# A table of offsets on the due times that order the instructions of a fused top-k attention and MLP kernel

## The chip, the cores and the metric

One core of a Trainium2 chip runs the kernel. The metric is the device time of one execution in microseconds (us), median of several runs. TensorE is called PE below, VectorE DVE, ScalarE ACT, GpSimd POOL; SyncE (SP) issues all DMAs of the kernel from one queue.

## The reference

```python
def _attn_ref(q, k, v):                      # q, k, v: (4, 8, 576, 64) float32
    scores = 1/sqrt(64) * matmul(q, k.T)
    kth = the 32nd largest of each row
    scores = where(scores >= kth, scores, -1e9); attn = softmax(scores)
    return matmul(attn, v)
def _moe_ref(x, w_in, w_out):                # x: (2304, 512); w_in (512, 2048), w_out (2048, 512)
    h = x @ w_in
    return (h * sigmoid(1.702 * h)) @ w_out
def _moe2_ref(x, w1, w2, w3, w_out):         # w1, w2: (512, 1024); w3 (1024, 1024); w_out (1024, 512)
    return ((x @ w1) * (x @ w2) @ w3) @ w_out
def reference(...):
    x = attention, heads joined to (2304, 512)
    return _moe2_ref(_moe_ref(x))
```

The weights arrive as 64-bit floats, the rest as 32-bit floats.

## The kernel before, in words

**Work.** The 2304 tokens are 18 tiles of 128. A tile has 8 heads. A head (`head`) is: scores `S` on PE into one of two PSUM buffers `s_ps` (L760); four `max` (L782) and three `mr` (match and replace, L785) on DVE, which find the 32nd largest score; `nb` (L792), a 128x1 operation that may run on POOL or on DVE; `cut` and `exp` on ACT (L800, L803); a split of the result into two fp16 parts, `a hi` on ACT (L809) and `a lo` on POOL (L812, L813); a DMA transpose `a T` (L816, into `ats`); and `av` on PE (L823). `tile_end` normalises the tile and transposes it (`x T`, L905, into `tsb`).

A tile then goes through `moe`: `h` products with `win`, tanh and a multiplication by ACT and POOL, a transpose `g T` (L973), `x2` products with `wout`, a transpose `x2 T` (L1010), products `a` and `b` with `w12`, their product, a transpose `p T` (L1077), products `o` with `w34` (w3 and the last weight, multiplied beforehand), and a store. All these products run in halves of six 128x512 fp16 matmuls (`product_op`, L532 to L534), eight halves for `h`, eight for `x2`, four for each of `a`, `b` and `o`.

**Weights.** Beside the first tiles, `weights` prepares 72 blocks of 128x512 in five stages: the last weight (8 blocks), w3 (16), w_in (16), w_out (16), w1 and w2 (16). `load64` loads a block (`w load`, L372), makes a 32-bit float of it with two ACT operations (`w low` L377, `w main` L391), one that may run on ACT or on POOL (`w sign`, L387 or L382), and one on DVE (`w join`, L395). `l2_scale` sums squares on PE (`gram`, L422) and derives a scale in DVE steps (`diag` L432, `w scale` L440, L441, L445, L446). `split_pe` copies a block through PSUM and splits it by that scale: `w in` on PE (L459), `w hi` on ACT (L462), `w lo` on DVE (L465). The 64-bit blocks of a later stage are loaded into memory that the split of an earlier stage frees, so the stages form a chain.

**What sets the order.** Class `Order` holds every operation with a due time `prio`, the engines that it may run on (`alts`: engine, cost, function, a wait `w` before that engine is considered), its dependencies and the buffers it takes and returns. `run` goes through planned time, and each time an engine is free it takes, of the operations that are ready in its plan, the one with the smallest due time. The costs are numbers in the code (`cost` in `pe`, `dve`, `act`, `pool`, `dma`). What the chip sees is only the resulting order on each of the five queues: each engine executes its list in that order, and waits by semaphores for the data itself. The due times come from `head_due`, which gives head n a time, with constants added for each kind:

```python
def head_due(n):
    return 9.0 * min(n, 16) + 5.7 * max(n - 16, 0) + 12.0
```

`S` and `av` get this time less 1000, so that PE takes them before any product.

Of the kernel before, what the change touches and what calls it, by code (L numbers as in the profile page):

```python
# [35 lines left out]
class Order:  # L36
# [22 lines left out]
    def op(self, alts, due, deps=(), env=None, acq=(), rel=(), tag="", lat=None):  # L59
        o = Op()  # L60
        o.alts, o.prio, o.lat = alts, due, lat
        o.acq = [(a, env, a) if isinstance(a, str) else a for a in acq]
        o.rel = [(a, env, a) if isinstance(a, str) else a for a in rel]
        o.left, o.users, o.ready, o.end, o.why = 0, [], 0.0, None, None
        o.tag, o.seq, o.done = tag, len(self.ops), False
        for d in deps:
            if d is not None:
                d.users.append(o)
                o.left += 1
        self.ops.append(o)  # L70
        return o
# [98 lines left out]
SIGN_G = 0.5  # L170

# [6 lines left out]
def kernel(  # L178
# [120 lines left out]
    def pe(cost, due, fn, **kw):  # L299
        return op([("T", cost, fn, 0.0)], due, **kw)  # L300
# [444 lines left out]

    def head(t, h, X):
# [85 lines left out]
        s = pe(0.5 if len(pt) == 1 else 0.65, due - 1000 - 8, f_s, deps=qready[t] + kd, env=E, acq=["sp"], rel=rel, tag="S")  # L832
# [8 lines left out]
        for i in range(3):  # L841
# [13 lines left out]
            0.55 if len(pt) == 1 else 0.75, due - 1000 + 10, f_av, deps=[tr] + vd + [X["av op", h - 1] if j else None],  # L855
# [3 lines left out]
        X["av op", h] = av
# [80 lines left out]
    def moe(t, X):  # L940
# [8 lines left out]
        gs = []  # L949
        for j in range(NG):  # L950
# [3 lines left out]
                [X["xt"]] + ready["win"][4 * j : 4 * j + 4], [("mm", E, "mm")], [("t", X, "t")] if j == NG - 1 else [], "h",  # L954
# [68 lines left out]
        ps_, pd = [], []  # L1023
        for j in range(NP_):
# [3 lines left out]
                [x2t] + ready["w12"][4 * j : 4 * j + 4], [("mm", Ea, "mm")], [], "a",  # L1028
# [120 lines left out]
```

## Time and profile before

| | |
|---|---|
| median of 3 runs | 1120.21 us (1118.58 to 1121.06) |
| the profiled execution | 1122.92 us, span 1121.1 us |
| PE, DVE, ACT, POOL busy | 987.4, 938.6, 833.6, 755.6 us |
| mean granted PE clock | 0.975 of full speed |

The span runs from the first to the last instruction of the profiled execution; times in the rows count from its start. A view of waits says which engine and line waited for which other. An entry PEld is PE's weight load, which goes ahead of its matmul. SPq is the DMA queue.

### The profile page before, as it was taken

To read this page: it belongs to the slowest core of one execution; us is meant where nothing else is said; L and a number is where in the kernel's file an instruction comes from. 1 tells how busy PE (TensorE), PEld (TensorE's weight loads), DVE (VectorE), ACT (ScalarE), POOL (GpSimd) and SP (SyncE) were. 2 spreads that over 40 slices of the span, in tenths; PEclk is the share of its full clock that TensorE was granted. 3 is DMA by queue.
4 is the path that set the end of the run, shared out by engine and by line. 5 is a ranking of instruction groups with operands and counts; after the bars stand their busy time and mean duration, and the time that the engine had idled before them with its cause. 6 is when DMAs were issued, how large, how long until landed. Compare 5 with 4: busy or idle time off the path is not lost.

```text
span 1121.1 us, 18684 instructions
## 1 busy us (share of the span) xinstructions
PE 987.4 (88%) x5798; PEld 504.9 (45%) x5798; DVE 938.6 (84%) x2079; ACT 833.6 (74%) x1589; POOL 755.6 (67%) x1092
## 2 busy tenths in 40 slices
PE   1367898688879999999999998999999999999995
PEld 1233343344434445555445454454445555455442
DVE  4798899699799999989999878998998999997311
ACT  6987858988978776878788687777777777777421
POOL 6733332555547886989798887878879796776320
PEclk9998999879989999999999999999999999999998
DMA  7969958768746675786776859576865664746331
GB/s 236 293 151 229 257 101 221 197 138 177 160 113 110 128 132 118 127 167 115 136 143 122 155 103 156 107 131 124 134 140 97 135 136 94 144 83 122 76 57 38
DMA packets 428740, 156.96 MB, mean 140 GB/s; under 512 B 406624, under 2 KB 414816, under 8 KB 428640
## 3 DMA queue, kind: packets, MB, share of 16 engines
q1 hardware_dynamic: 428640, 155.78, 67.6%
q8 instruction: 45, 0.74, 0.3%
q14 instruction: 55, 0.45, 0.1%
HBM read 52.43 MB, written 4.72 MB: 51 GB/s over the span
## 4 chain that ended last, share of the span: by engine, by line
PE 38%; DVE 16%; DMA 14%; ACT 12%; POOL 12%; issue 7%; SPq 1%; POOLq 0%; ACTq 0%; DVEq 0%
PE mm L532 10%; PE mm L534 10%; PE mm L533 10%; DVE m8s L782 7%; DVE wsb L785 6%; DMA ats<-hlb 5%; DMA tsb<-hsb 5%; PE av L823 4%; PE s_ps L760 3%; POOL hsb L343 2%; POOL hlb L813 2%; ACT ysb L803 2%; POOL hsb L935 1%; ACT s_ps L800 1%; PE mm L459 1%
## 5 line engine op out<-in xcount | busy, mean ns | idle before, releaser
L782 DVE MAX8 m8s<-wsb 128x8 f32<-128x576 f32 x432 | 323.6, 755 | 5.3
L785 DVE MATCH_REPLACE8 wsb<-m8s,wsb 128x576 f32<-128x576 f32 x288 | 213.8, 743 | 0.0
L532 PE MATMUL mm<-w,tsb 128*128 128x512 f16 x432 | 164.5, 381 | 12.8 <-DMA tsb<-hsb 10.2
L532 PEld LDWEIGHTS <-tsb 128*128 128x128 f16 x1072 | 105.2, 98 | 136.9 <-DMA tsb<-hsb 28.3
L813 POOL TENSOR_TENSOR hlb<-ysb,hlb 128x512 f16<-128x512 f32 x144 | 166.7, 1158 | 0.0
L534 PE MATMUL mm<-w,tsb 128*128 128x512 f16 x432 | 164.2, 380 | 0.0
L533 PE MATMUL mm<-w,tsb 128*128 128x512 f16 x432 | 164.2, 380 | 0.0
L534 PEld LDWEIGHTS <-tsb 128*128 128x128 f16 x1072 | 105.4, 98 | 128.8 <-issue 4.0
L533 PEld LDWEIGHTS <-tsb 128*128 128x128 f16 x1072 | 105.4, 98 | 116.0 <-issue 17.1
L532 PE MATMUL mm<-wout,tsb 128*128 128x512 f16 x352 | 134.0, 381 | 7.9 <-DMA tsb<-hsb 4.0
L782 DVE MAX8 m8s<-s_ps 128x8 f32<-128x576 f32 x144 | 109.1, 757 | 34.6 <-PE s_ps L760 29.6
L800 ACT ACTIVATE s_ps<-s_ps,m8s 128x576 f32<-128x576 f32 x144 | 102.5, 712 | 44.6 <-DVE m8s L782 36.8
L534 PE MATMUL mm<-wout,tsb 128*128 128x512 f16 x352 | 133.9, 380 | 0.0
L533 PE MATMUL mm<-wout,tsb 128*128 128x512 f16 x352 | 133.9, 380 | 0.0
L803 ACT ACTIVATE ysb<-s_ps,nbs,asm 128x576 f32<-128x576 f32 x144 | 119.7, 831 | 16.9 <-DVE nbs L792 10.6
L823 PE MATMUL av<-v2s,ats 128*128 128x130 f16 (+1 forms) x1440 | 105.7, 224 | 20.2 <-DMA ats<-hlb 17.1
L532 PE MATMUL mm<-win,tsb 128*128 128x512 f16 x288 | 111.6, 388 | 9.8 <-DMA tsb<-hsb 6.2
L760 PE MATMUL s_ps<-kts,qts 128*128 128x288 f16 (+1 forms) x640 | 101.0, 298 | 18.6 <-ACT ysb L803 15.4
L823 PEld LDWEIGHTS <-ats 128*128 128x128 f16 (+1 forms) x1440 | 90.2, 102 | 57.7 <-DMA ats<-hlb 29.6
L970 POOL TENSOR_TENSOR fsb<-fsb 128x512 f32<-128x512 f32 x68 | 87.0, 1279 | 38.1 <-ACT fsb L961 37.0
L533 PE MATMUL mm<-win,tsb 128*128 128x512 f16 x288 | 111.2, 386 | 0.0
L534 PE MATMUL mm<-win,tsb 128*128 128x512 f16 x288 | 111.2, 386 | 0.0
(182 smaller groups left out, 1877.8 us busy)
## 6 DMA issues: line engine op xcount, KB each, us to landing
w<-in_moe_w_dram SPq DMA_DIRECT2D x16, 512.0 KB, 6.8
wout<-in_moe_w_in_dram SPq DMA_DIRECT2D x16, 512.0 KB, 5.2
wout<-in_moe_w_out_dram SPq DMA_DIRECT2D x16, 512.0 KB, 4.5
qts<-qts SPq DMA_DIRECT2D x36, 128.0 KB, 2.4
out_dram<-fsb SPq DMA_DIRECT2D x18, 256.0 KB, 2.5
w<-in_moe_w_out_dram SPq DMA_DIRECT2D x8, 512.0 KB, 4.6
psb<-in_moe_w_dram SPq DMA_DIRECT2D x8, 512.0 KB, 4.8
tsb<-in_moe_w_dram SPq DMA_DIRECT2D x8, 512.0 KB, 5.6
```

Of the source, the lines that this page charges most:

```text
L343: nc.gpsimd.tensor_tensor(lo(), src(), hi(), op=ALU.subtract)
L532: nc.tensor.matmul(o, a[:, i, :], hi, start=(first and i == 0), stop=False)
L533: nc.tensor.matmul(o, a[:, i, :], lo, start=False, stop=False)
L534: nc.tensor.matmul(o, a[:, 4 + i, :], hi, start=False, stop=(last and i == 3))
L760: nc.tensor.matmul(E["sp"][r : r + n, i], qe[q_][:, h, r : r + n], kt[:, j, i * HS : (i + 1) * HS], start=k_ == 0, stop=k_ == 1,)
L782: nc.vector.max(out=E["m8"][:, 8 * i : 8 * i + 8], in_=E["sp"] if i == 0 else E["w"])
L785: nc.vector.match_replace(out=two(E["w"]) if i == 0 else E["w"], in_to_replace=E["m8"][:, 8 * i : 8 * i + 8], in_values=E["sp"] if i == 0 ...
L800: nc.scalar.activation(E["sp"], E["sp"], AF.Prelu, bias=E["m8"][:, TOPK - 1 : TOPK], scale=-1.0, alpha=1.0 / FAR)
L803: nc.scalar.activation(two(E["y"]), E["sp"], AF.Exp, bias=E["nb"], scale=nesc)
L813: nc.gpsimd.tensor_tensor(hl()[:, S + SR : 2 * S], E["y"][:, 0:SM], hl()[:, 0:SM], op=ALU.subtract)
L823: nc.tensor.matmul(X["av", hp][r : r + n, j], E["at"][:, i, r : r + n], v2[:, j, blk, :], start=(i == 0), stop=(i == 8))
L970: nc.gpsimd.tensor_tensor(E["f"], E["f"], E["f2"], op=ALU.mult)
```

## The change

Three things change in the code. First, a table `LATER` gives each kind of operation (its tag) eight offsets, for due times of -20 to 1000, and `later` interpolates between them; the offset is added to the due time. Second, a table `LONGER` changes the wait `w` of operations that have a choice of engines. Third, dependencies are added: each `S` follows the `S` before it, each `av` the `av` before it, each `h` product of a tile the one before, `a` the `b` before, `he` the `tanh`. No instruction of another kind is added and no tile is changed.

```diff
     def op(self, alts, due, deps=(), env=None, acq=(), rel=(), tag="", lat=None):
         o = Op()
-        o.alts, o.prio, o.lat = alts, due, lat
+        o.alts, o.prio, o.lat = [(e, c, f, max(w + LONGER.get((tag, e), 0.0), -1.0) if len(alts) > 1 else w) for e, c, f, w in alts], due + later(tag, due), lat
...
+TIMES = (-20, 60, 130, 220, 330, 500, 750, 1000)
+LATER = {
...
+    'w in': (33, -6, -44.5, -66.5, -24.5, -92, -110.5, -48.5),
...
+    'w scale': (-68.5, -13.5, 23, 25, -108.5, -85.5, -45, -123.5),
...
+LONGER = {
+    ('g hi', 'V'): 9.5, ('g hi', 'A'): -3, ('g lo', 'V'): 3.5, ('g lo', 'G'): -24.5, ('kv hi', 'V'): -1,
...
+def later(tag, due):
+
+    v = LATER.get(tag)
+    if v is None:
+        return 0.0
+    x = min(max(due + 1000 if due < -500 else due, TIMES[0]), TIMES[-1])
+    j = max(i for i in range(len(TIMES) - 1) if TIMES[i] <= x)
+    w = (x - TIMES[j]) / (TIMES[j + 1] - TIMES[j])
+    return v[j] * (1 - w) + v[j + 1] * w
...
-        s = pe(0.5 if len(pt) == 1 else 0.65, due - 1000 - 8, f_s, deps=qready[t] + kd, env=E, acq=["sp"], rel=rel, tag="S")
+        s = pe(0.5 if len(pt) == 1 else 0.65, due - 1000 - 8, f_s, deps=qready[t] + kd + [last_of.get("S")], env=E, acq=["sp"], rel=rel, tag="S")
...
-            0.55 if len(pt) == 1 else 0.75, due - 1000 + 10, f_av, deps=[tr] + vd + [X["av op", h - 1] if j else None],
+            0.55 if len(pt) == 1 else 0.75, due - 1000 + 10, f_av, deps=[tr] + vd + [last_of.get("av")],
...
-                [X["xt"]] + ready["win"][4 * j : 4 * j + 4], [("mm", E, "mm")], [("t", X, "t")] if j == NG - 1 else [], "h",
+                [X["xt"], pr] + ready["win"][4 * j : 4 * j + 4], [("mm", E, "mm")], [("t", X, "t")] if j == NG - 1 else [], "h",
...
-                he = act(0.48, due, f_he, deps=[pr], env=E, acq=[("f", E, "f2")], rel=["mm"], tag="he")
+                he = act(0.48, due, f_he, deps=[pr, ta], env=E, acq=[("f", E, "f2")], rel=["mm"], tag="he")
...
-                [x2t] + ready["w12"][4 * j : 4 * j + 4], [("mm", Ea, "mm")], [], "a",
+                [x2t, pb] + ready["w12"][4 * j : 4 * j + 4], [("mm", Ea, "mm")], [], "a",
```

Both programs have the same 5251 operations. Where an operation has a choice, the engine changes for some: 33 of the 72 `w sign` go from ACT to POOL, 30 of the 144 `nb` from POOL to DVE, 11 `p hi` go from POOL or DVE to ACT, and some ten others move. What moves in the order is shown at three places. In the rows of the change the line numbers are higher by about 110, for the same code.

DVE, where the scale of the first weight stage is derived, after `diag` (L432, in the change L540). In the order before, `diag` is row 60 of DVE, `w scale` (L440, L441, L445, L446) stands at rows 72, 76, 86 and 88 and the first `w lo` (L465, it writes `wout`) at row 92. The last part of it:

```order
L395 SCALAR_TENSOR_TENSOR win<-w_70,win 128x512
L792 TENSOR_SCALAR nbs<-m8s,asm 128x1
L445 TENSOR_SCALAR wsm<-wsm 128x1
L782 MAX m8s<-s_ps_94 128x8
L446 RECIPROCAL wsm<-wsm 128x1
L785 MATCH_REPLACE wsb<-m8s,s_ps_94 128x576
L782 MAX m8s<-wsb 128x8
L395 SCALAR_TENSOR_TENSOR win<-w_70,win 128x512
L465 SCALAR_TENSOR_TENSOR wout<-mm_97,wsm,wout 128x512
```

In the change `diag` is row 63, and the same steps are rows 65 to 74:

```order
L548 TENSOR_SCALAR wsm<-mm_97 128x1
L895 MATCH_REPLACE wsb<-m8s,wsb 128x576
L503 SCALAR_TENSOR_TENSOR win<-w_70,win 128x512
L549 TENSOR_SCALAR wsm<-wsm 128x1
L892 MAX m8s<-wsb 128x8
L553 TENSOR_SCALAR wsm<-wsm 128x1
L554 RECIPROCAL wsm<-wsm 128x1
L503 SCALAR_TENSOR_TENSOR win<-w_70,win 128x512
L892 MAX m8s<-s_ps_95 128x8
L573 SCALAR_TENSOR_TENSOR wout<-mm_99,wsm,wout 128x512
```

The scale and the first `w lo` moved ahead of some sixteen `max`, `mr` and `w join` of DVE, which now follow.

SP, where the third weight stage is first loaded (`in_moe_w_in_dram` into `wout`). Before, four loads stand behind two `a T` (into `ats`) and behind the two copies within `qts`:

```order
L724 DMA stg_84<-in_q_dram 128x8x64
L816 DMA_TRANSPOSE ats_78<-hlb_77 128x9x128
L698 DMA_TRANSPOSE kts_72<-hsb_81 128x4x128 x2
L701 DMA_TRANSPOSE kts_72<-kr16_86 128x2x64
L816 DMA_TRANSPOSE ats_78<-hlb_77 128x9x128
L733 DMA qts_74<-qts_74 64x1024
L734 DMA qts_74<-qts_74 64x1024
L372 DMA wout_69<-in_moe_w_in_dram 128x1024 x4
```

In the change:

```order
L832 DMA stg_84<-in_q_dram 128x8x64
L806 DMA_TRANSPOSE kts_72<-hsb_81 128x4x128 x2
L809 DMA_TRANSPOSE kts_72<-kr16_86 128x2x64
L480 DMA wout_69<-in_moe_w_in_dram 128x1024 x4
L926 DMA_TRANSPOSE ats_78<-hlb_77 128x9x128
```

The four loads moved ahead of one `a T` and of the copies, directly behind the third stage of `kts`.

PE, at the last `av` of the last tile. Before, half a `h` product (with `win`) follows it, and then the `x2` products of the tile before (with `wout`):

```order
L823 MATMUL av<-v2s,ats 128x130
L532 LDWEIGHTS tsb
L532 MATMUL mm_98<-win,tsb 128x512
L533 LDWEIGHTS tsb
L533 MATMUL mm_98<-win,tsb 128x512
```

In the change three halves of these `x2` products stand ahead of it, and the fourth directly behind:

```order
L933 MATMUL av<-v2s,ats 128x130
L640 LDWEIGHTS tsb
L640 MATMUL mm_99<-wout,tsb 128x512
L641 LDWEIGHTS tsb
L641 MATMUL mm_99<-wout,tsb 128x512
```

The last `av` moved behind four product halves that stood behind it (one of `h`, three of `x2`). From the first `x2` product of the last tile on, PE has the same order in both.

## Rows read from the trace of the kernel before

**Rows 1.** The page: busy time, share of the span and instructions of each engine.

```profile
PE 987.4 (88%) x5798; PEld 504.9 (45%) x5798; DVE 938.6 (84%) x2079; ACT 833.6 (74%) x1589; POOL 755.6 (67%) x1092
```

**Rows 2.** The view by stretches: stretch in us, its length, busy us of PE, PEld, DVE, ACT, POOL (instructions), then granted PE clock, DMA share, GB/s.

```profile
0.00:100.00 100.00, 42.58 (x221) 23.20 (x222) 74.79 (x167) 81.40 (x157) 55.42 (x93) 0.96 0.86 224
100.00:230.00 130.00, 104.46 (x575) 52.43 (x573) 111.16 (x214) 109.07 (x193) 53.26 (x72) 0.95 0.82 193
230.00:345.00 115.00, 98.49 (x500) 48.47 (x500) 101.43 (x220) 95.73 (x175) 63.43 (x91) 0.92 0.69 148
345.00:1030.00 685.00, 662.78 (x4136) 345.11 (x4135) 634.30 (x1445) 519.05 (x1013) 561.65 (x810) 1.00 0.68 127
1030.00:1090.00 60.00, 60.00 (x293) 27.79 (x292) 13.28 (x29) 23.64 (x46) 21.65 (x28) 1.00 0.36 70
1090.00:1121.00 31.00, 19.08 (x81) 7.87 (x79) 3.65 (x7) 4.71 (x9) 0.19 (x1) 0.87 0.18 43
```

**Rows 3.** The view of waits, 0 to 230 us: engine and line that waited, for whom; us in total, times, longest.

```profile
PEld L422 <- DVE w L395: 14.4, 15, 2.8
PEld L422 <- DVE wout L395: 13.3, 5, 5.1
PEld L422 <- DVE win L395: 11.2, 7, 3.5
```

**Rows 4.** The timeline of DVE, 53 to 77 us: start, us, engine, line, operation.

```profile
53.43 0.27 DVE L432 SCALAR_TENSOR_TENSOR mm<-mm,ident 128x128 f32<-128x128 f32 x1
...
63.27 0.14 DVE L440 TENSOR_SCALAR wsm<-mm 128x1 f32<-128x1 f32 x1
...
71.76 0.14 DVE L446 RECIPROCAL wsm<-wsm 128x1 f32<-128x1 f32 x1
...
73.51 1.99 DVE L395 SCALAR_TENSOR_TENSOR win<-w,win 128x512 uint32<-128x512 uint32 x1
75.42 0.74 DVE L465 SCALAR_TENSOR_TENSOR wout<-mm,wsm,wout 128x512 f16<-128x512 f32 x1
```

**Rows 5.** The timeline of the DMA queue, 84 to 92 us (time in the queue's hands, not the transfer).

```profile
83.10 1.28 SPq L816 DMA_TRANSPOSE ats<-hlb  x1
86.29 0.52 SPq L733 DMA_DIRECT2D qts<-qts  x1
86.86 0.59 SPq L734 DMA_DIRECT2D qts<-qts  x1
87.50 2.03 SPq L372 DMA_DIRECT2D wout<-in_moe_w_in_dram  x4
```

**Rows 6.** The groups of line L792 (`nb`) on DVE and on POOL: count, busy us, mean ns of one, idle time before them.

```profile
L792 DVE TENSOR_SCALAR nbs<-m8s,asm 128x1 f32<-128x1 f32 x53 | 13.8, 260 | 0.3
L792 POOL TENSOR_SCALAR nbs<-m8s,asm 128x1 f32<-128x1 f32 x91 | 36.7, 403 | 85.7 <-DVE m8s L782 60.0 <-DVE wsm L445 7.4 <-DVE msm L901 3.8
```

**Rows 7.** The lines of `w sign` on ACT (L387) and on POOL (L382) and of `w join` (L395): instructions, duration in ns min/median/max, first and last start; and the POOL timeline at 73 us.

```profile
L387 ACT ACTIVATE w<-wout x19: 756/776/817, 99.6 to 221.0; 128x512 f16<-128x512 f32 x19
L382 POOL TENSOR_SCALAR w<-wout x13: 762/773/1227, 92.7 to 223.9; 128x512 bf16<-128x512 f32 x13
L395 DVE SCALAR_TENSOR_TENSOR w<-wout,w x32: 673/684/1807, 96.6 to 227.2; 128x512 uint32<-128x512 uint32 x32
L395 DVE SCALAR_TENSOR_TENSOR win<-w,win x16: 667/691/1989, 42.8 to 84.5; 128x512 uint32<-128x512 uint32 x16
73.55 1.46 POOL L382 TENSOR_SCALAR win<-w 128x512 bf16<-128x512 f32 x2
```

**Rows 8.** The groups of `w join` (L395) on DVE: count, busy us, mean ns of one (two of five groups).

```profile
L395 DVE SCALAR_TENSOR_TENSOR w<-wout,w 128x512 uint32<-128x512 uint32 x32 | 26.7, 838 | 3.5 <-ACT wout L391 3.4
L395 DVE SCALAR_TENSOR_TENSOR win<-w,win 128x512 uint32<-128x512 uint32 x16 | 15.0, 948 | 2.4 <-ACT w L391 2.4
```

**Rows 9.** The view of waits, 345 to 1090 us: PE and its weight loads, and DVE.

```profile
DVE m8s L782 <- PE s_ps L760: 21.0, 23, 4.1
PEld L532 <- DMA tsb<-hsb: 13.7, 14, 2.6
PEld L823 <- DMA ats<-hlb: 11.1, 15, 1.6
PE mm L532 <- DMA tsb<-hsb: 9.4, 11, 2.3
```

**Rows 10.** The timeline of PE around the last `av` of tile 12 (808 us) and the first `h` product of that tile (826 us).

```profile
808.40 0.69 PE L823 MATMUL av<-v2s,ats 128*128 128x130 f16 x9
...
823.17 0.69 PE L760 MATMUL s_ps<-kts,qts 128*64 128x288 f16 x8
826.16 0.61 PE L532 MATMUL mm<-win,tsb 128*128 128x512 f16 x1 [2.30 <-DMA tsb<-hsb]
```

**Rows 11.** The timeline at the last `max`, the last `a T`, the last `av`, the last `x T` and the first `h` product of the last tile, from the timelines of DVE, SP and PE.

```profile
1028.35 0.76 DVE L782 MAX8 m8s<-wsb 128x8 f32<-128x576 f32 x1
...
1034.40 1.30 SPq L816 DMA_TRANSPOSE ats<-hlb  x1
1047.75 1.23 SPq L905 DMA_TRANSPOSE tsb<-hsb  x1
...
1038.07 0.69 PE L823 MATMUL av<-v2s,ats 128*128 128x130 f16 x9
...
1052.62 0.38 PE L534 MATMUL mm<-wout,tsb 128*128 128x512 f16 x1
1052.84 0.38 PE L532 MATMUL mm<-win,tsb 128*128 128x512 f16 x1
1053.05 0.38 PE L533 MATMUL mm<-win,tsb 128*128 128x512 f16 x1
```

**Rows 12.** The view of DMA issues: the transposes into `ats`, how many, and the median us from issue to landing; and, from the chain of work that ended last, the last transposes and the last ACT operation.

```profile
ats<-hlb SPq DMA_TRANSPOSE x144, 3.3
1106.76 3.32 DMA tsb<-hsb
...
1117.00 0.69 ACT fsb L1090
```

More of the change, by code (lines that the diff above doesn't have):

```diff
@@ L170 @@
 SIGN_G = 0.5
+TIMES = (-20, 60, 130, 220, 330, 500, 750, 1000)
+LATER = {
[12 rows of a table added]
+    'cut': (-8, -15.5, -2, 3, -9, -20.5, -11, -17),
+    'diag': (39.5, 2.5, 20.5, 65.5, 40, 45, 52, 66.5),
+    'diag sum': (-50, 21.5, 71, 59.5, 1, 0.5, -42, 5),
+    'esc': (-23, -21, -3.5, 9, -45, 4, 24.5, 50),
+    'exp': (-13.5, -46, -13.5, -2.5, -5, 9, 36.5, -10.5),
[4 rows of a table added]
+    'gram': (-11, -19.5, -21.5, 51.5, -6.5, 3.5, -21, -38.5),
[11 rows of a table added]
+    'max': (-2.5, 16.5, -1, 15.5, 24.5, 14, 69, 112),
[18 rows of a table added]
+    'store': (-22.5, -51.5, -129.5, -108, -76, -23, -32.5, -21),
+    'tanh': (-48, -15, 5, 16.5, 8, 116.5, 78, 4),
+    'th1': (9, -8, -85, -60.5, -67, -55, -25, -3),
+    'thsc': (-13.5, -18.5, -30.5, -35, 0.5, 14.5, -50.5, -79),
[27 rows of a table added]
+}
+LONGER = {
[6 rows of a table added]
+}
+def later(tag, due):
[6 more added lines that the diff above has]
+    return v[j] * (1 - w) + v[j + 1] * w
 def head_due(n):
@@ L743, in q_prep @@
         qready[t] = [dma(1.5, due, f_swap, deps=[tr], env=E, acq=[("q", E, "qb")], tag="q swap")]
+    last_of = {}
     def head(t, h, X):
@@ L854, in head @@
         av = pe(
[L855 removed]
+            0.55 if len(pt) == 1 else 0.75, due - 1000 + 10, f_av, deps=[tr] + vd + [last_of.get("av")],
             acq=[] if j else [("av", X, ("av", hp))], rel=[("at", E, "at")] + rel, tag="av",
         )
+        last_of["S"] = s
         X["S", h] = s
[L859 removed]
+        X["av op", h] = last_of["av"] = av
         if j == 1:
@@ L949, in moe @@
         gs = []
+        pr = None
         for j in range(NG):
@@ L973, in f_t @@
                 nc.sync.dma_start_transpose(out=E["t"], in_=E["h"])
-            a = act(0.58, due, f_th, deps=[pr, ths], env=E, acq=["f"], tag="tanh")
-            a = act(0.53, due, f_th1, deps=[a], tag="th1")
+            ta = act(0.58, due, f_th, deps=[pr, ths], env=E, acq=["f"], tag="tanh")
+            a = act(0.53, due, f_th1, deps=[ta], tag="th1")
             if tail or (t * NG + j) % 8 < G_DVE:
@@ L1023, in moe @@
         ps_, pd = [], []
+        pb = None
         for j in range(NP_):
```

75 rows, old and new, of tables (LATER, LONGER) are left out of this document.

## The prediction
> **What bounds the kernel now.** I read the page first: PE is busy 88% of the span and DVE 84%, no other engine above 74% [rows 1]. An average says little here, so the second view is the one by stretches [rows 2]; subtract busy time from length in it. From 345 us to 1090 us PE is idle 22.2 us in all (685.00 - 662.78, then nothing); from 1090 us 11.9; from 230 to 345 us 16.5; and from 0 to 230 us 83.0 us (57.4 and 25.5). So three quarters of the 133.7 us in which PE does nothing lie before 345 us, while weights are being prepared, and the rest of the program is close to a full PE. DVE is the second bound: its idle time is 25.2, 18.8, 13.6 and 50.7 us in the four stretches to 1030 us, 108 us together, and after 1030 us it has little to do. The last `max` begins at 1028.35 us, and the last `av` follows on PE at 1038.07 us [rows 11]. Heads, which run on DVE, and products, which run on PE, thus come out nearly even, and a change of order has to please both.
>
> The third view is that of waits. Early PE waits mostly for DVE: three rows of weight loads for `gram` behind `w join` add up to 38.9 us [rows 3]. In the middle PE waits for transposes: `tsb` 13.7 and `ats` 11.1 us by the weight loads' rows, while DVE waits 21.0 us for `S` from PE [rows 9]. These are the only amounts that an order of the middle can still win.
>
> **The change part by part.** The sum is made against the profiled execution: 1122.9 us, of which the span is 1121.1. The median of the runs, 1120.2, is 2.7 lower; the differences below are taken from that median at the end. A difference of 0.2% (2.2 us) is about what a measurement of this kernel can tell from no change.
>
> *The added dependencies.* They link operations of one engine to an earlier one of the same engine, and order the plan. They issue nothing. I cost them at 0; the engine runs its list in order anyway, so no cover is needed.
>
> *The first weight stage.* In the order before, the steps from `diag` at 53.43 to the last `w scale` at 71.76 us take 18.3 us, since `max`, `mr` and `w join` stand between them, and the first `w lo` comes at 75.42 [rows 4]. From `diag` to the first `w lo` there were 32 rows of DVE, 22 of them `max`, `mr` or `w join`; in the change there are 11, 6 of them large. Sixteen large rows fewer at about 0.7 us (a `max` takes 0.76 us, a short `w join` 0.67 [rows 7, 11]) bring the split forward by some 10 us. The lead is passed on by the queue: four loads for the third stage went out at 87.50 us, behind an `a T` at 83.10 and the copies of `qts` at 86.29 [rows 5]; in the change they stand ahead of these. So the third stage can start 7 to 10 us earlier, and the DMA engines, 0.86 busy in that stretch, have room. What is late instead is heads 4 to 9, whose `max` and `mr` stand behind the split; nothing waits for them then but PE's `av`, and PE is idle anyway.
>
> How much is left at 230 us, when PE fills up? DVE is busy 111.2 of the 130 us from 100 to 230 us [rows 2], and the order puts about the same DVE work in front of the fourth stage's last `w join` as before. A lead can therefore be kept only by cutting DVE's 18.8 us of idle time there. Ends: 0 and 10 us. I take 5, the middle, since neither row excludes an end. **-5 us.**
>
> *`w sign`.* 33 of them go from ACT (776 ns) to POOL (773 ns) [rows 7]. ACT, which is busy 81.4 of the first 100 us, loses 33 x 0.776 = 25.6 us of work; that is in the lead above. POOL, 55 and 53 us busy in 0 to 100 and 100 to 230, has room. What it may cost lies on DVE: the `w join` at 73.51 us took 1.99 us, beside 0.67 for the shortest, while two `w sign` ran on POOL from 73.55 for 1.46 us [rows 4, 7]. The groups' means are 0.84 and 0.95 us [rows 8], so 72 joins pay about 0.2 us each, 14 us, now. POOL's work before 345 us rises from 172.1 us [rows 2] by 25.5, 15%, and with it the overlap: 0.15 x 14 = 2.1 us of DVE. Ends: 0 and 25.5 us (each moved operation holding up a join for its whole length). I take 2, on DVE, where the lead covers it; without this cover it would go to the DVE side of the sum below. The Trainium skill, page "SBUF — State Buffer", section "Who interferes with whom", states that a DVE instruction with two SBUF inputs contends with a GpSimd instruction that reads SBUF, and that the later one blocks fully. By that rule taken alone the end of 25.5 us would be the estimate; this case's trace agrees on the mechanism (1.99 beside 0.67 us) but its joins pay far less on average.
>
> *`nb`.* 30 go from POOL (403 ns) to DVE (260 ns) [rows 6]: 30 x 0.26 = 7.8 us more work on DVE ahead of the last `max`. On POOL the 12.1 us go free, which is off the path. Hidden as long as DVE has idle time to give: see the sum.
>
> *The middle.* PE's 22.2 us of idle time from 345 to 1030 us are in short waits, as at 826.16: 2.30 us for `x T` [rows 10]. Between the last `av` of tile 12 and its first `h` there were 9 product halves at 6 x 0.215 = 1.29 us (pitch of [rows 11]), and there are 11 now: 2.6 us more to do while the transpose comes, so that wait should vanish. The same holds for most of the waits on `x2 T` and `p T`: for tile 8, from the last `b` to the first `o`, 10 halves where there were 6. But for tile 15, from `av` to `h`, there are 9 halves where there were 14, about 13 us with three heads' matmuls, and the same way took 12 to 13 us at its fastest, at the end (1038.07, landing about 1047.75 + 3.3 = 1051.05). Ends: all 22.2 us won, or some five tiles (6, 7, 11, 15 and 17 get less) each losing up to the 2.3 us of the longest such wait, 11.5 lost. I take 3 won, on the winning side but near no change, because gains are more numerous than losses and each is small. **-3 us.**
>
> *The clock.* PE's granted clock is 0.95 and 0.92 in 100 to 230 and 230 to 345 us [rows 2], and PE's busy time there would be 5 and 8 us shorter at full speed. The change fills PE's pauses no more than it moves them, and I take 0; the ends are -13 and +5.
>
> *The end.* Before, PE does not wait between the last `av` (1038.07) and the last tile's `h` (1052.84): 11 halves, 14.2 us, cover `x T`, which lands at about 1051.05, 13.0 us after the `av` began [rows 11, 12]. Now 9 halves do, 11.6 us, so with the `av`'s own 0.5 PE waits about 0.6 us. **+0.6 us.** From there on the order is the same, and the chain behind it (transposes at 1106.76, ACT at 1117.00 [rows 12]) keeps its length.
>
> **The sum** on PE: -5 - 3 + 0.6 = -7.4 us. DVE must agree. The last `av` began 0.4 us after its transpose landed (1034.40 + 3.3 = 1037.7 [rows 11, 12]). With four halves, 5.2 us, now ahead of it instead of behind, heads may end 5.2 + 0.4 - 0.6 = 5.0 us later at no loss. DVE carries 7.8 + 2.1 = 9.9 us more. So on the DVE side the end moves by 9.9 - 5.0 - s, where s is the idle time that DVE sheds. For -7.4 it must shed 12.3 of its 108 us. I expect that: about 5 in the preparation, and 7 of the 21 us in which it waits for `S` [rows 9] and of the pauses at weights. **Forecast: 1120.2 - 7 = 1113 us**, own range 1106 to 1118.
>
> **The rivals.**
> 1. *DVE ends last (slower).* If DVE sheds nothing, the end moves by +4.9 us; if the moved `w sign` block joins for half their length (13 us instead of 2), by +16. For it: DVE is already busy 634 of 685 us in the middle, and 30 `nb` are added to it. Against it: an order that starts weights earlier takes joins away from waiting. It decides once s is under 5. Middle of these: 1120.2 + 8 = 1128.
> 2. *The lead is kept whole.* -10 in the preparation, 10 won in the middle, and DVE sheds 25 us. For it: ACT loses 25.6 us of work in the very stretch where it is 0.8 busy. Against it: DVE's 108 us would have to fall by a quarter. 1120.2 - 20 = 1100.
> 3. *Nothing comes of it.* The order is made by planned costs, and waits are only exchanged: tile 15 loses what tile 12 wins, and at 230 us the same DVE work has been done at the same time. 1120 within 2.2.
>
> **How the numbers follow.** Chances: forecast 0.50, rival 1 0.22, rival 2 0.12, rival 3 0.16. The likeliest gives 1113. The range reaches from rival 2's 1100 to just short of rival 1's 1128: 1100 to 1127, which leaves out half of each, under 2 in 10. Faster by over 0.2%: 0.50 + 0.12 = 0.62; within: 0.16; slower: 0.22.
>
> **What would show it.** In the changed kernel's profile: `w scale` done some 10 us after `diag` and the third stage's first load out by 80 us; PE's idle time from 0 to 230 us down from 83 to about 78; PE's waits for `tsb` after 345 us below 13.7; the last `max` at or before 1027 us. Mean `w join` above 1.0 us, or a last `max` after 1033 us, would be rival 1. A third stage that starts early while `w lo` of w_out still starts around 230 us would show the lead lost, and the forecast wrong by its first term.

## The result and the profile after

The changed kernel takes **1090.54 us** (median of 4 runs, 1089.17 to 1092.31), the kernel before beside it 1120.63 (4 runs). The ratio is 0.974, 95% interval 0.971 to 0.977: 2.6% faster, 30 us. The forecast was 1113, from 1100 to 1127. The sign was right; the size was not, and the time lies 9 us below the range.

The page of the changed kernel, busy time by engine (the profiled execution took 1091.35 us, its span is 1089.3, its mean PE clock 0.976):

```profile
PE 982.2 (90%) x5798; PEld 504.8 (46%) x5798; DVE 931.9 (86%) x2104; ACT 827.2 (76%) x1572; POOL 769.3 (71%) x1086
```

The view by stretches, with the columns of [rows 2]; the last three end at the last `max`, 60 us later and at the end of the span, as there:

```profile
0.00:100.00 100.00, 49.63 (x276) 27.30 (x276) 76.67 (x174) 83.10 (x159) 64.75 (x104) 0.95 0.91 250
100.00:230.00 130.00, 108.09 (x556) 53.55 (x557) 114.47 (x233) 102.24 (x187) 77.66 (x103) 0.92 0.81 192
230.00:345.00 115.00, 102.59 (x562) 50.99 (x561) 109.39 (x233) 94.64 (x170) 69.91 (x101) 0.96 0.71 145
345.00:998.00 653.00, 642.51 (x4035) 337.22 (x4034) 619.10 (x1439) 513.41 (x994) 529.08 (x746) 1.00 0.70 130
998.00:1058.00 60.00, 60.00 (x294) 27.76 (x292) 9.12 (x24) 28.49 (x56) 27.66 (x34) 1.00 0.39 72
1058.00:1089.00 31.00, 19.43 (x82) 7.97 (x80) 3.17 (x6) 5.33 (x10) 0.20 (x1) 0.88 0.18 43
```

Subtract busy PE time from length in each row, as the prediction did, and the 31.8 us by which the span fell are accounted for to 0.2 us, the rounding of the last stretch:

| PE, us | before [rows 2] | after | difference | predicted |
|---|---|---|---|---|
| idle, 0 to 230 | 83.0 | 72.3 | -10.7 | -5 |
| idle, 230 to 345 | 16.5 | 12.4 | -4.1 | not costed |
| idle, 345 to the last `max` | 22.2 | 10.5 | -11.7 | -3 |
| idle, from there to the end | 11.9 | 11.6 | -0.3 | +0.6 |
| busy, whole span | 987.4 | 982.2 | -5.2 | 0 |

DVE, up to the last `max`, sheds idle time too: 108 us became 78. Its busy time up to there stayed about the same, 921.7 us before and 919.6 after, though 30 `nb` came to it. The last `max` and the last `av` of the changed kernel, from the timelines of DVE and PE:

```profile
998.07 0.76 DVE L892 MAX8 m8s<-wsb 128x8 f32<-128x576 f32 x1
...
1011.41 0.68 PE L933 MATMUL av<-v2s,ats 128*128 128x130 f16 x9
```

The `max` is 30.3 us earlier and the `av` 26.7 [rows 11]: the 3.6 us between lie in the product halves that now stand ahead of the `av`.

The first weight stage, DVE from `diag` (L540) to the first `w lo` (L573, into `wout`):

```profile
50.99 0.28 DVE L540 SCALAR_TENSOR_TENSOR mm<-mm,ident 128x128 f32<-128x128 f32 x1
...
55.04 0.16 DVE L554 RECIPROCAL wsm<-wsm 128x1 f32<-128x1 f32 x1
...
57.70 0.77 DVE L892 MAX8 m8s<-s_ps 128x8 f32<-128x576 f32 x1 [1.41 <-PE s_ps L870]
58.38 0.73 DVE L573 SCALAR_TENSOR_TENSOR wout<-mm,wsm,wout 128x512 f16<-128x512 f32 x1
```

From `diag` to the last `w scale` it is 4.1 us instead of 18.3, and the first `w lo` is 17 us earlier [rows 4]. The DMA queue of the changed kernel sends the third stage's first loads at 74.80 us, 12.7 earlier [rows 5]:

```profile
73.47 1.24 SPq L809 DMA_TRANSPOSE kts<-kr  x1
74.80 1.95 SPq L480 DMA_DIRECT2D wout<-in_moe_w_in_dram  x4
```

Waits of the changed kernel from 345 to 1058 us, to be read against [rows 9]: DVE waits 13.9 us for `S` instead of 21.0, and PE with its weight loads waits 7.7 us for `tsb` instead of 23.1. The waits for `ats` are as they were. The weight loads' share of these waits runs partly beside matmuls that are still busy, so not all of it is idle time of PE; the rows of PE alone for `tsb` are 9.4 before [rows 9] and 2.6 after.

```profile
DVE m8s L892 <- PE s_ps L870: 13.9, 20, 1.7
...
PEld L933 <- DMA ats<-hlb: 11.2, 16, 2.2
...
PEld L640 <- DMA tsb<-hsb: 5.1, 7, 1.1
```

```profile
PE mm L640 <- DMA tsb<-hsb: 2.6, 5, 0.8
```

Since both programs have the same operations, each can be found in both traces. This table gives start times in us; the same rows are used for the experiments.

| operation | before | after | earlier by |
|---|---|---|---|
| first third-stage load | 87.5 | 74.8 | 12.7 |
| last `w join` of stage four (block 55) | 227.2 | 217.7 | 9.5 |
| first `w lo` of w_out | 234.5 | 224.1 | 10.4 |
| last `w lo` of stage five | 345.9 | 332.0 | 13.9 |
| first `S` of tile 8 | 543.9 | 522.9 | 21.0 |
| first `S` of tile 12 | 742.7 | 714.5 | 28.2 |
| first `x2` product of tile 17 | 1076.1 | 1044.3 | 31.8 |

So a third of the gain is there at 230 us, under half at 345, and the rest comes after that, most of it before 750 us.

### The profile page after: what moved, and what is told of

It reads as the page before. It is cut to its first block, busy times and chain, and to the rows that moved or that the text cites. A ratio compares the mean times of both kernels' runs of the same rounds, so it can differ in the third digit from the quotient of the medians.

```text
span 1089.3 us, 18743 instructions
## 1 busy us (share of the span) xinstructions
PE 982.2 (90%) x5798; PEld 504.8 (46%) x5798; DVE 931.9 (86%) x2104; ACT 827.2 (76%) x1572; POOL 769.3 (71%) x1086
## 4 chain that ended last, share of the span: by engine, by line
PE 43%; DVE 16%; ACT 13%; POOL 10%; DMA 10%; issue 6%; SPq 1%; POOLq 0%; ACTq 0%; DVEq 0%
PE mm L640 11%; PE mm L642 11%; PE mm L641 11%; DVE m8s L892 7%; DVE wsb L895 6%; DMA ats<-hlb 5%; PE av L933 4%; PE s_ps L870 3%; DMA tsb<-hsb 3%; PE mm L567 2%; POOL hlb L923 2%; ACT ysb L913 2%; POOL hsb L451 1%; ACT hlb L919 1%; ACT s_ps L910 1%
## 5 line engine op out<-in xcount | busy, mean ns | idle before, releaser
L640 PE MATMUL mm<-wout,tsb 128*128 128x512 f16 x352 | 135.4, 385 | 4.6 <-ACT fsb L1079 2.5
L642 PE MATMUL mm<-wout,tsb 128*128 128x512 f16 x352 | 135.7, 385 | 0.0
L641 PE MATMUL mm<-wout,tsb 128*128 128x512 f16 x352 | 135.5, 385 | 0.0
L913 ACT ACTIVATE ysb<-s_ps,nbs,asm 128x576 f32<-128x576 f32 x144 | 119.9, 832 | 11.9 <-DVE nbs L902 4.7
L933 PE MATMUL av<-v2s,ats 128*128 128x130 f16 (+1 forms) x1440 | 104.7, 224 | 17.3 <-DMA ats<-hlb 17.0
L640 PE MATMUL mm<-win,tsb 128*128 128x512 f16 x288 | 109.8, 381 | 3.7 <-DMA tsb<-hsb 1.0
L1046 POOL TENSOR_TENSOR hsb<-fsb,hsb 128x512 f16<-128x512 f32 x72 | 84.4, 1174 | 37.5 <-ACT hsb L1040 25.7
L642 PE MATMUL mm<-win,tsb 128*128 128x512 f16 x288 | 109.9, 381 | 0.0
L641 PE MATMUL mm<-win,tsb 128*128 128x512 f16 x288 | 109.9, 381 | 0.0
L895 DVE MATCH_REPLACE8 wsb<-m8s,s_ps 128x576 f32<-128x576 f32 x144 | 107.6, 748 | 0.0
```

The costliest lines, as they stand in the source:

```text
L640: nc.tensor.matmul(o, a[:, i, :], hi, start=(first and i == 0), stop=False)
L641: nc.tensor.matmul(o, a[:, i, :], lo, start=False, stop=False)
L642: nc.tensor.matmul(o, a[:, 4 + i, :], hi, start=False, stop=(last and i == 3))
L895: nc.vector.match_replace(out=two(E["w"]) if i == 0 else E["w"], in_to_replace=E["m8"][:, 8 * i : 8 * i + 8], in_values=E["sp"] if i == 0 ...
L913: nc.scalar.activation(two(E["y"]), E["sp"], AF.Exp, bias=E["nb"], scale=nesc)
L933: nc.tensor.matmul(X["av", hp][r : r + n, j], E["at"][:, i, r : r + n], v2[:, j, blk, :], start=(i == 0), stop=(i == 8))
```

## The experiments

Times are medians, ratios are to the kernel before on the same chip, with 95% intervals. **The theory** after the result, which the runs bear out in part: ACT paces the preparation, and `w sign` on POOL relieves it; the new order turns this into a lead, and a lead is kept to the end; the middle gives the rest. **Rivals**: the tables pick one lucky order; the queue alone makes the lead; the gain is all of the front or all of the middle.

### Front and middle apart

The offsets are used only up to, or only from, a planned time; the added dependencies are in all four.

```diff
-                    mine = (o.prio + ...
+                    mine = ((o.prio if new(now) else o.base) + ...
+def new(now):
+    return now < 221.0       # x1_front220;  328 in x2_front345;  now >= 328 in x3_back345;  False in x4_deps_only
```

> The added dependencies stay. Until planned time 221 (about where the split of w_out starts on the chip) the tables rule the order, afterwards the old due times and waits do. Theory A (the lead of the preparation stays to the end): the split of w_out starts at about 221 us instead of 231, as in the changed kernel, and the end is 8 to 12 us earlier than before: about 1110 us. Theory B (PE and DVE come out even, so that a lead is only worth what the later order makes of it): the same lead at 221 us, but under 5 us of it left at the end: 1116 to 1121 us.

> The same with the switch at planned time 328, about where the last weight stage ends. Theory A: 14 to 20 us earlier than before, about 1103 us, so some 8 us more than with the switch at 221. Theory B: under 5 us, 1116 us or more. If the fifth stage gives nothing by itself, it comes out like the switch at 221.

> The reverse: the old order until planned time 328, the tables' order from there on. Theory A: no lead at 345 us, then 10 to 14 us won in the middle by fewer waits of PE for transposes and of DVE for scores: about 1108 us, and this gain and the one of the switch at 328 add up to the 30 us of the whole change. Theory B: the middle gives most, 20 us or more: 1100 us or less.

> The added dependencies alone, with the old due times and waits. Both theories: no change, within 3 us of the kernel before, 1118 to 1123 us. A change by more would mean that the dependencies, or any disturbance of the order, move the time by themselves.

| | us | ratio | first `w lo` of w_out | last `w lo` | first `S` of tile 12 |
|---|---|---|---|---|---|
| x1_front220 | 1112.62 | 0.993 (0.991 to 0.996) | 226.1 | 340.1 | 730.5 |
| x2_front345 | 1102.72 | 0.986 (0.983 to 0.989) | 224.5 | 332.7 | 721.3 |
| x3_back345 | 1119.74 | 1.001 (0.999 to 1.003) | 232.5 | 357.1 | 731.5 |
| x4_deps_only | 1128.63 | 1.009 (1.006 to 1.012) | 235.3 | 356.1 | 742.8 |

By the ratios the front up to 220 gives 8 us at the end for a lead of 8.4 at 230 us; up to 345, 16 for a lead of 13.2 in the last `w lo`. In these two a lead made early was not eaten by the middle; z4 and n3 below show that the end does not follow this landmark in general. The back alone shows nothing against the kernel before, where 10 to 14 us had been expected, but 9 us against x4, whose front is ordered by the same rules. Added to x4, front (26) and back (9) make 1094, near the 1090.5 measured. In the trace of x2, whose middle is ordered by the old rules, the first `S` of tile 8 comes at 523.2, as in the changed kernel (522.9), and that of tile 12 7 us later than there: up to tile 8 the tables of the middle added nothing to what the front had brought. Neither the rival "all front" nor "all middle" holds. Only the base they are added to is doubtful: each of these kernels is also another draw of the order, and how much a draw is worth is asked below. The runs of x1 spread from 1104 to 1119, so its median is the least firm.

### `w sign` alone, both ways

z1_sign_back is the changed kernel in its exact order on every queue, but each `w sign` runs on the engine that it had before. z5_sign_fwd is the reverse: the order before, and each `w sign` on the engine of the changed kernel. `back` holds the other kernel's engine of each `w sign`; the instructions are issued from `plan` afterwards. Place by place the engine differs for 43 of the 72: 38 go from ACT to POOL in the changed kernel and five the other way, 33 on balance.

```diff
-                a[2]()
+                plan.append((o, a))
...
+    return [(o, a if o.seq not in back else next(x for x in o.alts if x[0] == back[o.seq])) for o, a in plan]
```

> The changed kernel's order, row by row, but each of the 72 w sign operations runs on the engine that it had before: 42 places on ACT and POOL differ, nothing else moves. Theory A (ACT, back to back in the first 95 us, held the preparation, and moving w sign to POOL freed it): the leads shrink, the split of w_out starts some 5 us later than in the changed kernel, and the end comes 5 to 12 us later, at 1096 to 1102 us. Theory B (the order of DVE and of the loads made the lead, and w sign on POOL only holds up w join): the mean w join falls and the end is unchanged or up to 3 us earlier, 1088 to 1092 us.

> The kernel before, in its exact order; only each w sign runs on the engine that it has in the changed kernel (33 more on POOL). If ACT's relief alone makes the lead: the first w lo of w_out some 5 to 10 us before 234.5 us, and the end 5 to 10 us earlier, 1109 to 1114 us. If the lead needs the new order too (an order made for ACT's slower pace keeps the queue, DVE and POOL at that pace): first w lo of w_out within 3 us of 234.5, and the end within 4 us of the kernel before, 1115 to 1123 us, or later, since POOL's other work (a lo) then stands behind w sign.

| | us | ratio | first `w lo` of w_out | last `w lo` |
|---|---|---|---|---|
| z1_sign_back | 1101.20 | 0.984 (0.980 to 0.988) | 233.7 | 345.1 |
| z5_sign_fwd | 1123.30 | 1.003 (1.001 to 1.005) | 232.9 | 341.6 |

In z1 almost the whole lead of the preparation is gone (233.7 beside 234.5 before), and 10.7 us at the end. It is gone although the first loads of the third stage still go out 8.4 us earlier than in the kernel before:

```profile
79.10 1.95 SPq L501 DMA_DIRECT2D wout<-in_moe_w_in_dram  x4
```

So the rival that the queue alone makes the lead fails. What took the lead is in the groups of `w join` up to 230 us. First the changed kernel (count, busy, mean ns, idle before them and for whom), then z1_sign_back (L524 is `w join` there, L520 `w main` on ACT):

```profile
L503 DVE SCALAR_TENSOR_TENSOR w<-wout,w 128x512 uint32<-128x512 uint32 x32 | 26.1, 827 | 9.1 <-ACT wout L499 9.1
L503 DVE SCALAR_TENSOR_TENSOR win<-w,win 128x512 uint32<-128x512 uint32 x16 | 12.5, 797 | 0.4 <-ACT w L499 0.4
L503 DVE SCALAR_TENSOR_TENSOR wout<-w,wout 128x512 uint32<-128x512 uint32 x8 | 7.5, 944 | 3.4 <-ACT w L499 3.4
```

```profile
L524 DVE SCALAR_TENSOR_TENSOR w<-wout,w 128x512 uint32<-128x512 uint32 x32 | 25.2, 803 | 12.7 <-ACT wout L520 12.6
L524 DVE SCALAR_TENSOR_TENSOR win<-w,win 128x512 uint32<-128x512 uint32 x16 | 11.4, 726 | 4.0 <-ACT w L520 3.9
L524 DVE SCALAR_TENSOR_TENSOR wout<-w,wout 128x512 uint32<-128x512 uint32 x8 | 7.5, 944 | 5.1 <-ACT w L520 5.0
```

The joins wait 21.8 us for ACT instead of 12.9, 8.9 more, and are 2.0 us shorter in all (44.1 instead of 46.1), since fewer `w sign` run beside them on POOL. So in this order the relief of ACT is worth more than four times what the blocked joins cost. The order was made for `w sign` on POOL, though, so this is not the price of the same operations on ACT in an order made for that. And z5 shows that the relief alone buys nothing: under the order before, the first `w lo` of w_out moves by 1.6 us, the last by 4.3, and the median does not fall (the traced execution, 1117.45 us, is the fastest of ten). The view of waits of z5 up to 230 us, for DVE at `w join` (L416):

```profile
DVE wout L416 <- ACT w L412: 8.3, 5, 3.5
...
DVE w L416 <- ACT wout L412: 3.9, 5, 1.4
...
DVE win L416 <- ACT w L412: 2.8, 4, 0.9
```

That is 15.0 us. The kernel before shows 15.5 in the same three rows (9.7, 3.4 and 2.4), although ACT has 10.4 us less to do in z5 up to 230 us (180.1 instead of the 190.5 of [rows 2]). In that order ACT's list gives `w main` no sooner for being shorter: most of the time that is freed turns into other waits of ACT. Up to 230 us it waits 12.7 us for `w in` on PE (8.5 before), 5.3 for weight loads (2.0) and 3.7 for `w sign` on POOL (2.5). The second of the two expectations came, and the lead needs both edits.

### The place in the DMA queue

z3_loads_back puts the four first loads of the third stage behind the copies within `qts`; z4_loads_held holds back all work that depends on them (`behind`) or takes a buffer from such work (`dirty`) as well.

```diff
+    loads = [o for o in sorted((o for o, _ in plan if o.tag == "w load"), key=lambda o: o.seq)][24:28]
+    swap = sorted((o for o, _ in plan if o.tag == "q swap"), key=lambda o: o.seq)[1]
...
+        late = o.seq in behind or any((key2, slot) in dirty for key2, slot in slots[o.seq][0])
+        if late and not past:
+            held.append((o, a))
```

> The changed kernel's order with one move undone: the first four loads of the third weight stage stand on the DMA queue behind head 4's transpose and the two copies of the second tile's queries again, as before. Theory A (the queue passed the lead on): they go out some 8 us later than in the changed kernel, and the end is 4 to 10 us later, 1095 to 1100 us. Theory B (conversion by ACT and DVE holds the third stage, not its loads): the end moves by under 2 us.

In z3_loads_back the first conversions of that stage stand ahead of the loads and read the memory without waiting for them (the first at 77.2 us, the loads go out at 87.8), so its 1098.03 us do not say what the queue is worth. z4 asks again.

> The changed kernel's order, but the first four loads of the third weight stage, and all work of their blocks, are held back until the second pair of copies within qts (the place where the kernel before had them, one a T and two x T further). If the place in the DMA queue carries the lead (my prediction's step): the loads go out at about 88 to 90 us instead of 74.8, the first w lo of w_out comes at about 232 us instead of 224.1, and the end is 7 to 10 us later, 1098 to 1101 us. If ACT's relief from w sign carries it and the early loads only wait in memory: first w lo of w_out within 3 us of 224.1, and the end within 3 us of 1090.5.

1096.64 us, ratio 0.979 (0.976 to 0.983). Its DMA queue:

```profile
89.32 0.55 SPq L869 DMA_DIRECT2D qts<-qts  x1
89.92 0.60 SPq L870 DMA_DIRECT2D qts<-qts  x1
90.57 2.02 SPq L508 DMA_DIRECT2D wout<-in_moe_w_in_dram  x4
```

The loads go out at 90.57, 15.8 us later, and the first `w lo` of w_out comes at 232.0, 7.9 later than in the changed kernel, as the queue theory says. The end was 6 us later by the median, a little under the 7 to 10 expected. So without the early loads, and the work that hangs on them, the lead at 230 us is gone; with early loads but `w sign` on ACT, as z1 shows, it is gone too. The later part of the theory, that a lead lost is lost for good, does not hold in the one execution that was traced: it took 1092.90 us, the fastest of the four, and has made up all but about 1 us by tile 14 (815.6 beside 814.5). The other three runs, 1096 to 1098, have no trace, so where they lost it stays open.

### `nb`

z2_nb_back is the changed kernel's order with each `nb` on its engine of before: 53 on DVE instead of 83.

```diff
+        if o.tag == 'nb':
+            back[o.seq] = None
...
+    return [(o, a if o.seq not in back else next(x for x in o.alts if x[0] == back[o.seq])) for o, a in plan]
```

> The changed kernel's order, row by row, but each nb runs on the engine that it had before: 53 on DVE instead of 83. Theory A (DVE's work counts to the end, since heads and products come out even): 30 x 0.26 = 7.8 us less on DVE, the end 3 to 6 us earlier, about 1086 us. Theory B (an nb that queues on POOL behind operations of over 1 us holds up exp, and with it the score buffer for the head after next): exp waits longer for nb, the end 3 to 12 us later, about 1098 us.

1096.63 us, ratio 0.981 (0.977 to 0.985): in the changed kernel's order the 30 `nb` on DVE are worth 6 us, where the prediction feared a cost of 7.8 us of DVE. `exp` on ACT waits for them. The group of `exp` in z2_nb_back, then in the changed kernel, then in the kernel before:

```profile
L934 ACT ACTIVATE ysb<-s_ps,nbs,asm 128x576 f32<-128x576 f32 x144 | 119.8, 832 | 28.5 <-POOL nbs L923 21.6 <-DVE nbs L923 4.0
```

```profile
L913 ACT ACTIVATE ysb<-s_ps,nbs,asm 128x576 f32<-128x576 f32 x144 | 119.9, 832 | 11.9 <-DVE nbs L902 4.7 <-POOL nbs L902 2.7 <-POOL v2s L451 0.8
```

```profile
L803 ACT ACTIVATE ysb<-s_ps,nbs,asm 128x576 f32<-128x576 f32 x144 | 119.7, 831 | 16.9 <-DVE nbs L792 10.6 <-POOL nbs L792 2.9 <-DVE msm L997 0.4
```

From z2 to the changed kernel ACT's idle time behind `nb` falls from 25.6 to 7.4 us. In the kernel before, with the same engines as z2, it was 13.5: part of the 25.6 comes from an order that was made for `nb` on DVE, so how much of the 30 us is due to `nb` is not shown. On POOL an `nb` takes 414 ns, beside 259 on DVE, and shares its queue with `a lo`, 1.4 us each; on DVE it stands in the queue of the `max` that it needs. How the 18 us divide between these was not traced.

### One lucky order?

A planned cost is changed by one hundredth of a microsecond, which changes no rule and still reorders the program: the planned cost of a product half is 1.30 instead of 1.31 (n1, n6, n3), or that of `mr` 0.76 instead of 0.75 (n2, n7).

```diff
-        x = pe(1.31, due, lambda: part(0, 2), deps=deps, acq=acq, tag=tag)
+        x = pe(1.30, due, lambda: part(0, 2), deps=deps, acq=acq, tag=tag)
```

> A neutral disturbance: the kernel before, with the planned cost of a product half set to 1.30 instead of 1.31; no offsets, no dependencies, no work changed. It only makes the planner come to another order of the same kind. If the time depends on the rules alone: within 3 us of before. If each order is a draw: up to 10 us either way, and the 8 us that the added dependencies cost by themselves are such a draw.

> The kernel before, with the planned cost of mr 0.76 instead of 0.75: a second neutral disturbance of the order. If the order before is a good draw: slower by 0.3 to 1%, as n1_cost_130. If n1 was a poor draw: within 0.3%.

> The added dependencies alone (as x4_deps_only), with the disturbance of n1_cost_130. If the dependencies cost nothing by themselves: within 4 us of n1's ratio of 1.006, that is 1122 to 1130 us. If they cost the 0.9% of x4: 1.015, about 1135 us.

> The added dependencies alone, with the disturbance of n2_cost_076. If the dependencies cost nothing by themselves: within 4 us of n2_cost_076. If they cost 0.9%: 10 us above n2_cost_076.

> The changed kernel with its tables, but the planned cost of a product half is 1.30 instead of 1.31: the same rules, another draw of the order, as n1_cost_130 was for the kernel before. If what the tables bring holds for any order made with them, the time rises as n1's did, by 0.3 to 1%, to 1094 to 1101 us. If the tables only pick one lucky order out of many, most of the 30 us is lost: 1108 to 1122 us.

| us (ratio) | as it is | 1.30 | 0.76 |
|---|---|---|---|
| kernel before | 1118 to 1121 | n1: 1125.24 (1.006) | n2: 1122.37 (1.003) |
| with the dependencies | x4: 1128.63 (1.009) | n6: 1116.77 (0.997) | n7: 1137.45 (1.016) |
| with dependencies and tables | 1090.54 (0.974) | n3: 1090.40 (0.974) | |

The dependencies alone range from -0.3% to +1.6% as the order is redrawn. By the ratios n6 is 10 us faster than n1, and n7 15 us slower than n2. So neither expectation on them held: they have no price of their own that these runs could tell from the scatter of the order, which is some 10 us either way with them. The order before is the fastest of the three draws of its rules. The tables are no lucky draw in this sense: redrawn once, they give the same time (n3), where a loss of 0.3 to 1% or of most of the gain had been expected. The order differs, though: in n3 the first `w lo` of w_out comes at 231.9 and the last at 339.9, both nearly 8 us later than in the changed kernel, but the first `S` of tile 8 at 522.8 and that of tile 12 at 711.7, as early or earlier. So what the heads and the end get does not hang on these landmarks of the weights alone.

Much of this scatter is already in the plan. The planned end that `run` returns is 1101.4 for the kernel before, 1101.4 for n1 and 1104.6 for n2; 1106.8 for x4, 1095.1 for n6 and 1116.5 for n7; 1070.1 for the changed kernel and 1072.6 for n3. The exceptions are n1, for which no loss was planned, and x3, planned at 1093.7 and not faster than before.

The tables without the dependencies give no kernel: the planner comes to a point at which no operation can go.

### Other tables

v4_tables and v1_tables have other numbers in both tables, found by two separate walks of small random steps that kept what made the kernel's own plan end earlier. Nothing else is changed.

```diff
-    'h': (45.5, 25.5, -5.5, -9.5, -17.5, -25.5, -44, 13.5),
+    'h': (198, -17, 66.5, 3.5, -22, -28, -49, 47.5),
```

> The changed kernel with other numbers in both tables, moved in small steps so that the kernel's own plan ends earlier (planned 1055.8 instead of 1070.1). If the chip follows the plan as it did from the kernel before to the changed one (30 us for 31 planned): 1076 to 1080 us. If the plan's last per cents are fitted to planned costs that the chip doesn't have: 1087 to 1096 us.

> As v4_tables, with numbers from another such walk (planned 1055.8 too). Same two theories: 1076 to 1080 us, or 1087 to 1096 us. If the two kernels lie far apart (over 6 us) at the same planned end, the plan's end is no guide at this size.

v4 takes **1075.09 us** (ratio 0.960, 0.957 to 0.964) and v1 1076.80 (0.962, 0.958 to 0.965): 4% faster than the kernel before, and 14 to 15 us faster than the changed kernel. The first theory held, that the chip follows the plan; v4 lies 1 us below its range. v4 by stretches, cut nearly as above (its last `max` begins at 981.7):

```profile
0.00:100.00 100.00, 46.67 (x259) 27.15 (x260) 75.10 (x173) 84.20 (x162) 64.49 (x102) 0.93 0.88 243
100.00:230.00 130.00, 111.99 (x578) 55.21 (x576) 116.73 (x241) 106.75 (x190) 67.78 (x91) 0.93 0.80 192
230.00:345.00 115.00, 101.54 (x597) 50.80 (x598) 109.44 (x236) 96.85 (x181) 78.20 (x115) 1.00 0.72 157
345.00:984.00 639.00, 631.29 (x3973) 331.73 (x3972) 608.82 (x1417) 510.41 (x989) 534.73 (x757) 1.00 0.71 131
984.00:1044.00 60.00, 60.00 (x293) 27.64 (x291) 9.90 (x25) 22.27 (x45) 19.77 (x26) 1.00 0.34 63
1044.00:1072.00 28.00, 22.69 (x105) 9.89 (x103) 3.17 (x6) 7.04 (x13) 4.18 (x6) 0.98 0.28 66
```

PE's idle time falls to 7.7 us in the middle and 5.3 behind the last 60 us; in all 97.8 beside 106.8. The other half of the 17 us by which the span is shorter is PE's busy time, 974.2 beside 982.2, at a clock of 1.00 instead of 0.96 from 230 to 345 us and 0.98 instead of 0.88 at the end. Reckoned as in the prediction, busy time times the missing share of the clock, the clock costs PE 11.6 us in v4 and 17.6 in the changed kernel, an estimate that gives it 6 of these 8 us. Most of the idle time that is left lies ahead of 230 us: 71 of the 98 us.

## Why the prediction was wrong, and where it was right

1. **The lead of the first stage: seen, and halved without need.** The prediction found the 18.3 us between `diag` and `w scale`, the loads behind the copies, and a lead of about 10 us; the first `w lo` came 17 us earlier and the load 12.7, more than written, and a lead of 10.4 was left at 230 us. Then it took 5, the middle of 0 and 10, because DVE has the same work ahead of the fourth stage's last `w join`. That premise held. The view by stretches from the start to that `w join`, before and after (columns as in [rows 2]):

```profile
0.00:227.20 227.20, 145.46 (x785) 74.47 (x785) 183.18 (x372) 187.67 (x343) 106.40 (x161) 0.96 0.84 208
```

```profile
0.00:217.70 217.70, 146.21 (x787) 75.07 (x788) 180.03 (x376) 175.97 (x326) 132.18 (x192) 0.95 0.85 220
```

   DVE is busy 183.2 and 180.0 us in them, ACT 187.7 and 176.0. The step that failed is the next one, that DVE's idle time would give only half. It gives 6.3 us (44.0 to 37.7), and the 3.2 us of work make up the 9.5. Where the 6.3 come from stands in the views of waits up to 230 us, before and after:

```profile
DVE wout L395 <- ACT w L391: 9.7, 6, 3.5
DVE m8s L782 <- PE s_ps L760: 8.5, 7, 3.7
```

```profile
DVE m8s L892 <- PE s_ps L870: 4.1, 5, 2.1
DVE wout L503 <- ACT w L499: 3.4, 4, 1.8
```

   The wait for `S` gives 4.4, and the three rows of `w join` behind ACT only 2.6 (15.5 to 12.9); part of the latter stood in [rows 8], in the last column. So against the kernel before, the joins' wait for ACT is the smaller part. That the lead still hangs on ACT is shown the other way round: z1 puts `w sign` back on ACT, the joins wait 8.9 us longer, and the lead is gone. The prediction counted ACT's 25.6 us as "in the lead above" without asking whether the lead hangs on them.
2. **Stage five was left out.** From 230 to 345 us PE's idle time fell by 4.1 us, and the last `w lo` comes 13.9 us earlier, not 10.4. [rows 2] showed 16.5 us idle there, and no term spoke of it. x1 against x2 prices the tables of this stretch at 8 us of the end by the ratios and 10 by the medians.
3. **`w sign` beside joins: the size right, in part by luck.** 2 us were predicted; z1 against the changed kernel shows 2.0 us of join time up to 230 us, and the mean `w join` (0.87 us before, 0.83 after) is far from rival 1's 1.0. Rival 1's end, joins blocked for half their length, did not come. But the reckoning, that the joins' loss grows with POOL's work, failed between the two kernels: POOL had 33 more `w sign`, and the 72 joins took 58.9 us instead of 62.4.
4. **`nb`: the sign was wrong.** Costed as 7.8 us of DVE, hidden; undone in the new order, it costs 6 us. The term looked at the engine that gets the work, and not at ACT, which waits for the result.
5. **The middle: mis-sized.** -3 of 22.2 was taken; it was -11.7, between the forecast and the end of -22. The waits named were the right ones: for `tsb` 23.1 fell to 7.7, for `S` 21.0 to 13.9. The loss feared at the tiles with fewer halves did not come. Between the last `av` and the first `h` of tile 15 the halves fell from 14 to 9 as written, and PE does not wait there; at the tiles 6, 7, 11, 15 and 17 together it waits 0.54 us before the first `h`, all of it at tile 6, where up to 2.3 each were set. The wait of 2.30 us at tile 12 [rows 10] is down to 0.47:

```profile
801.19 0.39 PE L640 MATMUL mm<-win,tsb 128*128 128x512 f16 x1 [0.47 <-DMA tsb<-hsb]
...
932.12 0.38 PE L640 MATMUL mm<-win,tsb 128*128 128x512 f16 x1
```

6. **The clock: 0, and nothing else is shown; PE's busy time: not costed, and -5.2 came.** The granted clock rose from 0.92 to 0.96 between 230 and 345 us, but fell from 0.95 to 0.92 between 100 and 230. By the prediction's own reckoning, busy time times the missing share of the clock, it costs PE 17.3 us before and 17.6 after, an estimate from the two views by stretches; over the span it is 0.975 and 0.976. So by these rows the clock's 0 stands, and what made PE's busy time shorter by 5.2 us stays open.
7. **The dependencies: 0**, and the runs give no other number, only a scatter of some 10 us either way that the prediction had not allowed for. Redrawn without any purpose, the order before moves by 3 to 6 us, and the one with the dependencies by 8 to 14 (by the ratios); its 2.2 us for "no change" and the whole sum of -7.4 are of that size.
8. **The end: about right.** +0.6 was predicted and PE does not wait at all there; heads do end later against the products, by 3.6 us where 5.0 were allowed.
9. **DVE's side: mis-sized too.** The sum had 9.9 us more work on DVE and asked it to shed 12.3 us of idle time. Its busy time up to the last `max` fell by 2.1 us, and it shed 29.9.

Terms 1, 2, 5, 6 and 8 differ by 5.7, 4.1, 8.7, 5.2 and 0.9 us from what came, all the same way: 24.6, which with the -7.4 makes the 32 us by which the span fell. Rival 2, the lead kept whole, 10 us won in the middle, DVE shedding a quarter of its idle time (28% it was), came nearest and had a chance of 0.12; its 1100 is still 9.5 us too long, for the terms 2 and 6. That all errors lie on one side suggests that they were not independent, the terms having been set near the middle of their ends one by one; no run shows by what they hang together.

## What to carry to other kernels

When a lead is found on a chain, ask which engine paces the rest of that chain, two waits back, before taking half of it: if the change also relieves that engine, the lead can be kept. A landmark on that chain is not yet the end: n3 reached the same end with its weights nearly 8 us later. An edit of engines and an edit of order made by the same planner are one edit; each alone may be worth nothing, as `w sign` was under the old order, and taking one back in an order made for it prices both. In a list-scheduled kernel redraw the order once or twice without purpose, since a difference below that scatter (here about 1%) says nothing about the rule that made it, and read the planned end beside it.

## What the runs showed of the hardware that was not expected

Joins beside more `w sign` on POOL became shorter on the whole (0.870 to 0.827 us on average), though 33 more of them ran there; in the same order they lengthen by 2.0 us over 56 joins. So here the order in which POOL's work meets the joins counted for more than its amount. And a single profile can mislead on a kernel whose runs spread: z4's traced run lay 4 us below the median of the four, and its landmarks from tile 14 on would have shown a loss of 1 us.
